# Cluster attention and two token mixers: idle matmuls among the first maxima, the second clusters' rows earlier, value products and row sums of group 0 regrouped

## The chip, the cores and the metric

The kernel runs on one NeuronCore of a Trainium2 chip. Its engines are TensorE (PE; PEld is its weight load), VectorE (DVE), ScalarE (ACT), GpSimd (POOL) and SyncE (SP, which issues the DMAs here). The metric is the device time of one launch in microseconds; smaller is better.

## The reference, cut to what matters

```python
# q, k, v: (2, 8, 768, 64); centroids: (8, 16, 64)
q_assign = argmax(q_n . c_n);  k_assign = argmax(k_n . c_n)       # cluster of each row
mask = q_assign[:, :, :, None] == k_assign[:, :, None, :]
scores = where(mask, (q @ k^T) / 8, -1e9)
attn = exp(scores - max(scores)); attn /= (sum(attn) + 1e-9)
x = (attn @ v), heads side by side                                # (2, 768, 512)
theta = x @ w_theta; y = w_tok_r @ (x cos theta) + w_tok_i @ (x sin theta)
u = x + y; x = u + relu(u @ w_ch)                                 # first mixer
u = x + (x^T U V)^T; out = u + relu(u @ w_ch1) @ w_ch2            # second mixer
```

## The kernel before, in words

The sixteen (batch, head) pairs are worked in eight groups of two heads. For a group g the inputs are loaded (`load_raw`), split into a high and a low part (`split_hi` L188 on ScalarE, `split_lo` L193 on GpSimd) and packed by sixteen DMAs (`pack`, L213) into the operands `qp` and `kp`. `assign_items` finds the clusters: similarities on TensorE (`sims` L121), then a transpose, a maximum (`amax` L128), four small operations and a transpose back on VectorE. The resulting one-hot rows become extra rows of `qp` and `kp`, by DMA (`mask_rows`, L161) or, for groups 0 and 1, directly through TensorE (`mask_direct`: products `oht` L174, copies on ScalarE L177, L179 and VectorE L181).

Row maxima come first: `max_pair(g, h, a)` multiplies two query tiles of head h with all keys, in three parts of one PSUM bank each (`smax` L251), and VectorE reduces each part (L255). `max_join` and `max_rows` put the maxima as rows into the second operand `qp[s, h, 1]`: a small product `mrow` (L281) and two ScalarE copies (L284). Only then can `scores_pair(g, h, a)` be finished: every part is a sum of two products, the second of them with `qp[s, h, 1]` (L303), and ScalarE takes its exponential (L308). `pv` multiplies with the values (L316) and `sum_keys(g, a)` gives half of the row sums (L335, then a transpose on VectorE, L338).

`prologue` does group 0's clusters, all its maxima and the scores of its head 0, and starts groups 1 and 2. Its function `heat(n)` issues n matmuls of 512 columns on a tile of zeros into a bank that nobody reads (L935). `attention` runs for each group six slots p = 0 to 5. In a slot stand the scores of group g, the maxima of group g + 1, and background work: `fill(t)` adds t to a debt `owed` and takes items from the queue `bg` (input split, pack, clusters of group g + 2; each with a cost), then weight conversion steps (`conv_step`; `magnitude` L385 on ScalarE waits for a weight block from HBM), until the debt is paid. t is 4.8 in the slots `BURST` = (2, 5) and 0.3 in the others. Value products and row sums stand in slots 2 and 5. `max_rows(g, 1)` stands in slot 2 of group g, behind the background work.

Each engine works its instructions in the order in which the code issues them. PSUM banks go round: `bank()` takes the one that was taken longest ago, and `give` returns those that were kept.

Of the kernel before, what the change touches and what calls it, by code (L numbers as in the profile page):

```python
# [41 lines left out]
def tile_cluster_block(ctx: ExitStack, tc: tile.TileContext, qk, v, cent, wth, wr, wi, wch,  # L42
                       u_in, v_in, w1, w2, cst, out):
    nc = tc.nc
# [194 lines left out]
    mx_t = {}  # L239
    THIRDS = [[(0, 0, 512)], [(0, 512, 256), (1, 0, 256)], [(1, 256, 512)]]  # L240

    def max_pair(g, h, a):

        s = g % SETS
        if a == 0:
            mx_t[g, h] = small.tile([P, 2 * NT], F32, tag="mx12", name="mx12")
        o = 2 * a
        for part in THIRDS:
            ps, c = bank("smax"), 0
            for j, k0, w in part:  # L250
                nc.tensor.matmul(out=ps[:, c:c + w], lhsT=qp[s, h, 0][:, (a + j) * P:(a + j + 1) * P],  # L251
                                 rhs=kp[s, h, 0][:, k0:k0 + w], start=True, stop=True)
                c += w
            n = len(part)
            nc.vector.tensor_reduce(mx_t[g, h][:, o:o + n], ps.rearrange("p (n w) -> p n w", n=n), axis=AX.X, op=ALU.max)  # L255
            o += n

    def max_join(g, h, act=False):
        mx = small.tile([P, NT], F32, tag="mx", name="mx")
# [68 lines left out]
    def sum_keys(g, a):  # L328

        ps = bank("l")  # L330
        for kt in range(3 * a, 3 * a + 3):
            for h in range(2):
                for hf in range(2):
                    o = 32 * (2 * h + hf)
                    nc.tensor.matmul(out=ps[o:o + 32, :HALF], lhsT=ones, rhs=pt[g, h, kt][:, cols(hf)],  # L335
                                     start=(kt == 3 * a), stop=(kt == 3 * a + 2))
        lt = slot("lt")[:, :HALF]
        nc.vector.transpose(lt, ps[:, :HALF])  # L338
        lsum[g, a] = lt
# [472 lines left out]
    assign = {}  # L812
# [21 lines left out]
    def attention():  # L834
# [1 line left out]

        ORDER = [(0, 0), (0, 2), (0, 4), (1, 0), (1, 2), (1, 4)]
        BURST = (2, 5)
        pvq = deque()
        held[0] = True  # L840

        def next_pv():
# [5 lines left out]
        for g in range(NG):  # L848
# [20 lines left out]
            if not nxt:  # L869
                for t in range(NP):  # L870
                    bg.append((1., lambda t=t: split_x(0, t, nc.gpsimd)))
            order = [(1, 0), None, (1, 2), None, (1, 4), None] if g == 0 else ORDER
            for p in range(NT):
                ready = len(pvq)
                if order[p]:
                    h, a = order[p]
                    scores_pair(g, h, a)
                    if h:
                        pvq.extend((g, kt, hf) for kt in (a, a + 1) for hf in range(2))
                if g == 0 and p < 2:  # L880
                    mask_direct(1, p, nc.scalar if p else nc.vector)
                if nxt:
                    max_pair(g + 1, p // 3, 2 * p % 6)
                    if p % 3 == 2:
                        max_join(g + 1, p // 3)

                while conv_after:
                    conv_after.popleft()()
                if p == 3 and g + 2 < NG:
                    mask_rows(g + 2)  # L890
                if g > 0 and p == 5:
                    bg.appendleft((.95, lambda: norm_x(g - 1)))
                    bg.appendleft((.97, lambda: spread(g - 1)))
                fill(2. if not nxt else 4.8 if p in BURST else .3)
                if not nxt:
                    if p == 0:
                        sum_keys(g - 1, 1)
                    if p == 2:
                        max_rows(g, 1)
                    if p == 5:  # L900
                        sum_keys(g, 0)
                    for _ in range(min(ready, (2, 2, 2, 0, 4, 4)[p])):
                        next_pv()
                elif p in BURST:
                    if p == 2 and g > 0:
                        max_rows(g, 1)
                        sum_keys(g - 1, 1)
                    if p == 5:
                        max_rows(g + 1, 0)
                        sum_keys(g, 0)  # L910
                    for _ in range(min(ready, 6)):
                        next_pv()
                    if p == 5 and g + 3 < NG:
                        (_, sims), *assign[g + 3] = assign_items(g + 3)
                        sims()
                if g > 0 and p == 2:
                    row_sums(g - 1)
# [9 lines left out]
    def prologue():  # L927
# [43 lines left out]
            for it in items:  # L971
                it[1]()

        its, its1 = assign_items(0), assign_items(1)
        for i in range(2):
            split_hi(0, i)
        split_lo(0, 0, nc.gpsimd)
# [10 lines left out]
        run(its[1:])  # L988
        run(its1[:1])
        mask_direct(0, 0, nc.vector)  # L990
        mask_direct(0, 1, nc.scalar)
        split_lo(0, 1, nc.gpsimd)
        pack_low(0, (0, 1))
        for i in range(2):
# [2 lines left out]
        pack_direct(1, 0)  # L997
        pack(1, main=(1,))
        pack_low(1, (0,))
        for a in (0, 2, 4):  # L1000
            max_pair(0, 0, a)
        max_join(0, 0, act=True)
        max_pair(0, 1, 0)
        max_pair(0, 1, 2)
        max_rows(0, 0)
        init_packs(2, nc.gpsimd)
        scores_pair(0, 0, 0)
        max_pair(0, 1, 4)
        max_join(0, 1)
        run(its1[1:])  # L1010
        scores_pair(0, 0, 2)
        heat(2)
        scores_pair(0, 0, 4)
        heat(2)
        max_rows(0, 1)
        its2 = assign_items(2)
        run(its2[:4])
        assign[2] = its2[4:]
        give("hot")

    def mixer():
# [171 lines left out]
```

## Time and profile before

| | us |
|---|---|
| median of 3 runs (684.31, 685.65, 945.77) | 685.65 |
| profiled execution, device time | 684.24 |
| its span in the trace | 682.4 |
| TensorE busy | 669.9 |
| VectorE busy | 464.7 |
| ScalarE busy | 348.6 |
| GpSimd busy | 272.0 |

The span is shorter than the device time by 1.84 us, which lies around it. The prologue ends at about 30 us, group 0 at 52.5, group 1 at 76.5; from there on TensorE has next to no idle time, so what an earlier stage loses or gains shows in full at the end.

### The profile page before, as it was taken

Reading aid. Unit: us, or ns where it says so; the run is one execution under the profiler, and the core shown is the slowest. Engines: PE = TensorE matmul, PEld = TensorE weight load, DVE = VectorE, ACT = ScalarE, POOL = GpSimd, SP = SyncE. Lnnn points to the kernel's source line nnn. Section 1 sums busy time; section 2 is a strip of 40 time slices with the busy share of each in tenths; the row PEclk is TensorE's granted clock in tenths of the full one; section 3 lists DMA queues with packets and bytes.
Section 4 is the critical chain, followed back from the end, with each engine's and each line's share of the span. In section 5 each row is a group of like instructions: output and inputs, shape, how many; then the busy total and the mean of one; then the engine's idle time right before and its main releaser. Section 6 shows DMA issues by size and latency. Waiting matters only on the chain.

```text
span 682.4 us, 11870 instructions
## 1 busy us (share of the span) xinstructions
PE 669.9 (98%) x4563; PEld 573.7 (84%) x4564; DVE 464.7 (68%) x832; ACT 348.6 (51%) x713; POOL 272.0 (40%) x277
## 2 busy tenths in 40 slices
PE   8899999999999999999999999999999999999997
PEld 3567766755765599999999999798899999999997
DVE  6888887897876366547374766777387765776554
ACT  8647656665776554455464442334354534543221
POOL 9423323223236333114234102348555765656321
PEclk9799999999999999999999999999999999999999
DMA  6769788476522102003120220112222211210013
GB/s 206 206 148 273 194 192 245 152 186 168 169 94 93 47 1 78 2 1 109 47 78 12 70 71 1 46 32 78 78 77 63 79 53 71 62 32 1 0 48 139
DMA packets 21833, 63.15 MB, mean 93 GB/s; under 512 B 4272, under 2 KB 7216, under 8 KB 21776
## 3 DMA queue, kind: packets, MB, share of 16 engines
q1 hardware_dynamic: 21776, 62.39, 31.3%
q8 instruction: 36, 0.59, 0.3%
q14 instruction: 21, 0.17, 0.1%
HBM read 40.94 MB, written 3.15 MB: 65 GB/s over the span
## 4 chain that ended last, share of the span: by engine, by line
PE 90%; ACT 5%; DVE 4%; DMA 1%; issue 1%; SPq 0%; ACTq 0%
PE y L562 15%; PE acc L801 15%; PE q L749 13%; PE pv L316 9%; PE st L303 8%; PE h L580 5%; PE l L335 5%; PE th L520 5%; PE acc L722 5%; PE g L703 4%; PE smax L251 3%; DVE mx L255 2%; ACT p L308 2%; PE h L631 2%; ACT hi L188 1%; PE th L524 1%
## 5 line engine op out<-in xcount | busy, mean ns | idle before, releaser
L401 POOL TENSOR_TENSOR wl<-cv,wh 128x768 fp32r<-128x768 f32 (+1 forms) x33 | 57.3, 1736 | 129.8 <-ACT wh L397 108.4
L255 DVE TENSOR_REDUCE mx<-smax 128x1 f32<-128x512 f32 x144 | 89.5, 680 | 21.9 <-PE smax L251 21.9
L308 ACT ACTIVATE p<-st 128x512 f32<-128x512 f32 x192 | 79.1, 513 | 44.5 <-PE st L303 43.7
L801 PE MATMUL acc<-g,wh 128*128 128x384 f32 x384 | 97.5, 334 | 0.0
L562 PE MATMUL y<-wh,z 128*128 128x384 f32 x384 | 87.6, 340 | 0.3 <-ACT z L540 0.3
L763 POOL TENSOR_TENSOR g<-sum,g 128x384 fp32r<-128x384 f32 x48 | 53.0, 1103 | 82.1 <-ACT g L762 76.2
L757 DVE TENSOR_TENSOR xT<-acc,xT 128x384 f32<-128x384 f32 x96 | 53.0, 555 | 42.0 <-PE acc L801 41.7
L303 PE MATMUL st<-qp,kp 128*128 128x256 f32 (+1 forms) x384 | 79.8, 350 | 0.4 <-ACT qp L284 0.2
L303 PEld LDWEIGHTS st<-qp,kp 128*128 128x128 f32 x384 | 58.6, 193 | 19.0 <-issue 8.5
L801 PEld LDWEIGHTS acc<-g,wh 128*128 128x128 f32 x384 | 69.4, 188 | 0.0
L562 PEld LDWEIGHTS y<-wh,z 128*128 128x128 f32 x384 | 66.9, 188 | 0.5 <-ACT z L540 0.5
L316 PE MATMUL pv<-p,v 128*32 128x384 f32 x768 | 66.2, 486 | 0.0
L761 ACT ACTIVATE sum<-sum 128x384 f32<-128x384 f32 x48 | 25.2, 524 | 78.5 <-DVE sum L757 78.5
L757 DVE TENSOR_TENSOR sum<-q,sum 128x384 f32<-128x384 f32 x84 | 45.5, 553 | 28.0 <-PE q L749 22.0
L801 PE MATMUL acc<-g,wl 128*128 128x384 f32 x192 | 64.1, 334 | 0.0
L316 PEld LDWEIGHTS pv<-p,v 128*32 128x32 f32 x768 | 31.5, 110 | 29.5 <-issue 20.9
L546 POOL TENSOR_TENSOR z<-tht,z 128x256 fp32r<-128x256 f32 x24 | 19.3, 803 | 86.2 <-ACT z L540 86.1
L392 DVE SCALAR_TENSOR_TENSOR cv<-cv,st 128x768 int32<-128x768 int32 (+2 forms) x47 | 50.4, 1072 | 3.0 <-ACT cv L385 2.6
L562 PE MATMUL y<-wl,z 128*128 128x384 f32 x192 | 48.8, 335 | 0.0
L251 PE MATMUL smax<-kp,qp 128*128 128x512 f32 x192 | 43.9, 347 | 3.0 <-ACT qp L177 1.9
L251 PEld LDWEIGHTS smax<-kp,qp 128*128 128x128 f32 x192 | 32.9, 191 | 12.9 <-issue 4.3
L385 ACT ACTIVATE cv<-st 128x768 f32<-128x768 f32 (+2 forms) x47 | 38.9, 827 | 5.3 <-POOL wl L475 3.6
(170 smaller groups left out, 1461.4 us busy)
## 6 DMA issues: line engine op xcount, KB each, us to landing
st<-in_w_dram SPq DMA_DIRECT2D x17, 512.0 KB, 3.4
st<-in_w_dram SPq DMA_DIRECT2D x10, 768.0 KB, 4.0
raw<-in_qk_dram SPq DMA_DIRECT2D x16, 384.0 KB, 4.8
qp<-hi SPq DMA_DIRECT2D x26, 192.0 KB, 2.9
st<-in_wr_dram SPq DMA_DIRECT2D x6, 768.0 KB, 4.5
st<-in_wi_dram SPq DMA_DIRECT2D x6, 768.0 KB, 4.2
kp<-hi SPq DMA_DIRECT2D x32, 96.0 KB, 3.1
qp<-lo SPq DMA_DIRECT2D x32, 96.0 KB, 2.8
```

The lines of the kernel that those rows point to most:

```text
L251: nc.tensor.matmul(out=ps[:, c:c + w], lhsT=qp[s, h, 0][:, (a + j) * P:(a + j + 1) * P], rhs=kp[s, h, 0][:, k0:k0 + w], start=True, stop=True)
L255: nc.vector.tensor_reduce(mx_t[g, h][:, o:o + n], ps.rearrange("p (n w) -> p n w", n=n), axis=AX.X, op=ALU.max)
L303: nc.tensor.matmul(out=ps[:, c:c + n], lhsT=kp[s, h, w][:, (a + j) * P:(a + j + 1) * P], rhs=qp[s, h, w][:, q0:q0 + n], start=(w == 0), st ...
L308: nc.scalar.activation(out=pt[g, h, a + j][:, q0:q0 + n], in_=ps[:, c:c + n], func=AF.Exp, scale=float(D) ** -0.5)
L316: nc.tensor.matmul(out=pvt[g][hf][r:r + 32, :HALF], lhsT=v_t[g][:, kt, r:r + 32], rhs=pt[g, r // 64, kt][:, cols(hf)], start=(kt == 0), st ...
L392: nc.vector.scalar_tensor_tensor(t, t, 3, self.lw, op0=ALU.logical_shift_left, op1=ALU.bitwise_or)
L401: nc.gpsimd.tensor_tensor(t[:, :c.w], c.t, f32(c.hi[:, :c.w]), op=ALU.subtract)
L562: nc.tensor.matmul(out=yps[u, j][hf][:, :HALF], lhsT=lhs, rhs=w[st][e][:, hf * HALF:(hf + 1) * HALF], start=(st == 0 and n == 0), stop=(st ...
L749: nc.tensor.matmul(out=ps[:, :HALF], lhsT=w[a][:, j * P:(j + 1) * P], rhs=u_block(self.b, y, e, j), start=(n == 0), stop=(n == 5))
L757: nc.vector.tensor_tensor(out, ps[:, :HALF], x, op=ALU.add)
L763: nc.gpsimd.tensor_tensor(t[:, 1], r, f32(t[:, 0]), op=ALU.subtract)
L801: nc.tensor.matmul(out=ps[:, :HALF], lhsT=wv[a], rhs=self.g[i, hf][:, x], start=(m == 0), stop=(m == 5))
```

## The change

In the prologue, four idle matmuls are put ahead of the first maxima and one behind each of twelve parts of the maxima of group 0; four idle matmuls between later scores go. The maximum of group 1's similarities is taken ahead of the first maxima, group 2's similarities ahead of `max_rows(0, 1)`. The scores (0, 1, 0) and the direct mask rows of group 1 move from group 0's first slots into the prologue. In group 0 the other scores stand in slots 1 and 3, four value products each in slots 1, 3 and 5, and both halves of the row sums in slots 3 and 5; group 1's slot 2 loses its row sums and value products.

```diff
--- before.py
+++ after.py
@@ -239,7 +239,7 @@
     mx_t = {}
     THIRDS = [[(0, 0, 512)], [(0, 512, 256), (1, 0, 256)], [(1, 256, 512)]]
 
-    def max_pair(g, h, a):
+    def max_pair(g, h, a, warmer=None):
 
         s = g % SETS
         if a == 0:
@@ -254,6 +254,8 @@
             n = len(part)
             nc.vector.tensor_reduce(mx_t[g, h][:, o:o + n], ps.rearrange("p (n w) -> p n w", n=n), axis=AX.X, op=ALU.max)
             o += n
+            if warmer:
+                warmer(1)
 
     def max_join(g, h, act=False):
         mx = small.tile([P, NT], F32, tag="mx", name="mx")
@@ -836,7 +838,7 @@
 
         ORDER = [(0, 0), (0, 2), (0, 4), (1, 0), (1, 2), (1, 4)]
         BURST = (2, 5)
-        pvq = deque()
+        pvq = deque((0, kt, hf) for kt in (0, 1) for hf in range(2))
         held[0] = True
 
         def next_pv():
@@ -869,7 +871,7 @@
             if not nxt:
                 for t in range(NP):
                     bg.append((1., lambda t=t: split_x(0, t, nc.gpsimd)))
-            order = [(1, 0), None, (1, 2), None, (1, 4), None] if g == 0 else ORDER
+            order = [None, (1, 2), None, (1, 4), None, None] if g == 0 else ORDER
             for p in range(NT):
                 ready = len(pvq)
                 if order[p]:
@@ -877,8 +879,6 @@
                     scores_pair(g, h, a)
                     if h:
                         pvq.extend((g, kt, hf) for kt in (a, a + 1) for hf in range(2))
-                if g == 0 and p < 2:
-                    mask_direct(1, p, nc.scalar if p else nc.vector)
                 if nxt:
                     max_pair(g + 1, p // 3, 2 * p % 6)
                     if p % 3 == 2:
@@ -901,14 +901,16 @@
                         sum_keys(g, 0)
                     for _ in range(min(ready, (2, 2, 2, 0, 4, 4)[p])):
                         next_pv()
-                elif p in BURST:
-                    if p == 2 and g > 0:
+                elif p in (BURST if g else (1, 3, 5)):
+                    if p == 2:
                         max_rows(g, 1)
-                        sum_keys(g - 1, 1)
+                        if g > 1:
+                            sum_keys(g - 1, 1)
                     if p == 5:
                         max_rows(g + 1, 0)
-                        sum_keys(g, 0)
-                    for _ in range(min(ready, 6)):
+                    if p == 5 or p == 3:
+                        sum_keys(g, int(g == 0 and p == 5))
+                    for _ in range(min(ready, 6 if g else 4)):
                         next_pv()
                     if p == 5 and g + 3 < NG:
                         (_, sims), *assign[g + 3] = assign_items(g + 3)
@@ -971,7 +973,7 @@
             for it in items:
                 it[1]()
 
-        its, its1 = assign_items(0), assign_items(1)
+        its, its1, its2 = assign_items(0), assign_items(1), assign_items(2)
         for i in range(2):
             split_hi(0, i)
         split_lo(0, 0, nc.gpsimd)
@@ -988,7 +990,9 @@
         run(its[1:])
         run(its1[:1])
         mask_direct(0, 0, nc.vector)
+        run(its1[1:2])
         mask_direct(0, 1, nc.scalar)
+        heat(4)
         split_lo(0, 1, nc.gpsimd)
         pack_low(0, (0, 1))
         for i in range(2):
@@ -997,25 +1001,26 @@
         pack_direct(1, 0)
         pack(1, main=(1,))
         pack_low(1, (0,))
-        for a in (0, 2, 4):
-            max_pair(0, 0, a)
+        max_pair(0, 0, 0)
+        max_pair(0, 0, 2, heat)
+        max_pair(0, 0, 4, heat)
         max_join(0, 0, act=True)
-        max_pair(0, 1, 0)
-        max_pair(0, 1, 2)
+        max_pair(0, 1, 0, heat)
+        max_pair(0, 1, 2, heat)
         max_rows(0, 0)
         init_packs(2, nc.gpsimd)
         scores_pair(0, 0, 0)
         max_pair(0, 1, 4)
         max_join(0, 1)
-        run(its1[1:])
+        run(its1[2:])
         scores_pair(0, 0, 2)
-        heat(2)
         scores_pair(0, 0, 4)
-        heat(2)
+        run(its2[:2])
         max_rows(0, 1)
-        its2 = assign_items(2)
-        run(its2[:4])
-        assign[2] = its2[4:]
+        scores_pair(0, 1, 0)
+        mask_direct(1, 0, nc.vector)
+        mask_direct(1, 1, nc.scalar)
+        assign[2] = its2[3:]
         give("hot")
 
     def mixer():
```

The first place is TensorE's order in the prologue behind the direct mask rows of group 0. Before:

```order
L174 LDWEIGHTS identb
L174 MATMUL oht<-eqw,identb 16x384
L251 MATMUL smax<-kp_87,qp_85 128x512
L251 MATMUL smax<-kp_87,qp_85 128x256 x2
L251 MATMUL smax<-kp_87,qp_85 128x512 x2
L251 MATMUL smax<-kp_87,qp_85 128x256 x2
L251 MATMUL smax<-kp_87,qp_85 128x512 x2
L251 MATMUL smax<-kp_87,qp_85 128x256 x2
L251 MATMUL smax<-kp_87,qp_85 128x512
L251 MATMUL smax<-kp_91,qp_89 128x512
```

Now (`hot` is the tile of zeros):

```order
L937 LDWEIGHTS hot
L937 MATMUL hot<-hot 128x512
L251 MATMUL smax<-kp_87,qp_85 128x512
L251 MATMUL smax<-kp_87,qp_85 128x256 x2
L251 MATMUL smax<-kp_87,qp_85 128x512 x2
L937 LDWEIGHTS hot
L937 MATMUL hot<-hot 128x512
L251 MATMUL smax<-kp_87,qp_85 128x256 x2
L937 LDWEIGHTS hot
L937 MATMUL hot<-hot 128x512
```

What moved: idle matmuls stand ahead of the first part and, from the second pair on, behind each part.

The second place is ScalarE's order in group 1, from slot 2's last exponential to slot 3's first (`hi` is the input split, `cv` a converted weight block, `mrow` the maxima rows, `xT` the copy of the value products). Before:

```order
L308 ACTIVATE p_820<-st 128x512
L385 ACTIVATE cv<-st 128x768
L284 ACTIVATE qp_98<-mrow 2x384 x2
L323 ACTIVATE xT_893<-pv 128x384 x2
L308 ACTIVATE p_908<-st 128x512
```

Now:

```order
L310 ACTIVATE p_832<-st 128x512
L188 ACTIVATE hi_0_863<-raw_0_514 128x768
L188 ACTIVATE hi_1_865<-raw_1_516 128x768
L387 ACTIVATE cv<-st 128x768
L286 ACTIVATE qp_98<-mrow 2x384 x2
L310 ACTIVATE p_919<-st 128x512
```

What moved: the two splits stood behind slot 0's exponentials; now they stand in slot 2, ahead of the copies of the maxima rows. The value products' copy is gone from here.

The third place is TensorE's order at the same point of group 1 (`l` are the row sums). Before:

```order
L281 MATMUL mrow<-identb,m_668 2x128
L335 MATMUL l<-p_404,ones 32x384 x2
L335 MATMUL l<-p_557,ones 32x384 x2
L335 MATMUL l<-p_422,ones 32x384 x2
L335 MATMUL l<-p_629,ones 32x384 x2
L335 MATMUL l<-p_423,ones 32x384 x2
L335 MATMUL l<-p_630,ones 32x384 x2
L316 MATMUL pv<-p_423,v_192 32x384 x2
L316 MATMUL pv<-p_630,v_192 32x384 x2
L316 MATMUL pv<-p_423,v_192 32x384 x2
L316 MATMUL pv<-p_630,v_192 32x384 x2
L303 MATMUL st<-qp_97,kp_99 128x512
```

Now:

```order
L283 LDWEIGHTS m_711
L283 MATMUL mrow<-identb,m_711 2x128
L305 MATMUL st<-qp_97,kp_99 128x512
L305 MATMUL st<-qp_98,kp_100 128x512
L305 MATMUL st<-qp_97,kp_99 128x256
L305 MATMUL st<-qp_98,kp_100 128x256
```

What moved: the row sums and value products between the maxima rows and the next scores are gone; they stand in group 0.

## Rows read from the trace of the kernel before

**Rows 1.** The page: span; busy time, share and count of each engine.
```profile
span 682.4 us, 11870 instructions
...
PE 669.9 (98%) x4563; PEld 573.7 (84%) x4564; DVE 464.7 (68%) x832; ACT 348.6 (51%) x713; POOL 272.0 (40%) x277
```

**Rows 2.** Stretches: start:end, length, busy per engine, granted clock, DMA share, GB/s.
```profile
13.30:19.50 6.20, 5.30 (x20) 3.17 (x20) 5.64 (x10) 4.87 (x9) 6.14 (x6) 1.00 0.90 292
19.60:26.30 6.70, 6.07 (x22) 4.60 (x23) 5.57 (x10) 3.02 (x8) 5.37 (x8) 0.50 0.95 207
...
33.10:34.30 1.20, 0.02 (x1) 0.05 (x1) 0.97 (x2) 1.18 (x3) 0.00 (x0) 1.00 0.00 0
```

**Rows 3.** Timeline, VectorE, maxima: start, length, operation, count, [idle before, releaser].
```profile
13.77 5.47 DVE L255 TENSOR_REDUCE mx<-smax 128x1 f32<-128x512 f32 x9 [0.72 <-PE smax L251]
...
24.48 1.89 DVE L255 TENSOR_REDUCE mx<-smax 128x1 f32<-128x512 f32 x3 [1.01 <-PE smax L251]
...
26.81 0.17 DVE L271 TENSOR_TENSOR m<-mx,m 128x6 bf16<-128x6 f32 x1
...
65.39 3.70 DVE L255 TENSOR_REDUCE mx<-smax 128x1 f32<-128x512 f32 x6
```

**Rows 4.** Timeline, TensorE: the prologue and group 0, same columns.
```profile
7.12 3.19 PE L935 MATMUL hot<-hot 128*128 128x512 bf16 x14
...
13.26 5.94 PE L251 MATMUL smax<-kp,qp 128*128 128x512 f32 x20 [0.71 <-ACT qp L177]
...
21.51 2.50 PE L303 MATMUL st<-qp,kp 128*128 128x512 f32 x7 [0.18 <-ACT qp L284]
...
30.36 1.97 PE L303 MATMUL st<-qp,kp 128*128 128x512 f32 x8
...
34.28 0.94 PE L251 MATMUL smax<-kp,qp 128*128 128x512 f32 x4 [1.20 <-ACT qp L177]
...
39.01 2.79 PE L316 MATMUL pv<-p,v 128*32 128x384 f32 x32
```

**Rows 5.** Chain of waits, end of group 0 and group 1: start, length, what.
```profile
51.82 0.65 PE sims L121 x8
...
54.75 1.40 PE st L303 x8
...
58.63 0.69 PE smax L251 x4
...
59.59 1.94 PE l L335 x22
61.53 1.29 PE pv L316 x16
62.82 1.15 PE st L303 x6
...
71.94 3.87 PE pv L316 x48
```

**Rows 6.** Timeline, ScalarE, group 1: exponentials, input split, weight block, maxima rows.
```profile
53.23 1.64 ACT L308 ACTIVATE p<-st 128x512 f32<-128x512 f32 x4 [6.18 <-PE st L303]
54.73 1.60 ACT L188 ACTIVATE hi<-raw 128x768 fp32r<-128x768 f32 x2
...
60.68 0.95 ACT L385 ACTIVATE cv<-st 128x768 f32<-128x768 f32 x1 [1.30 <-DMA st<-in_wth_dram]
61.53 0.96 ACT L284 ACTIVATE qp<-mrow 2x384 fp32r<-2x384 f32 x2
```

**Rows 7.** Timeline, SyncE's queue in group 1: packs and one-hot rows of group 3.
```profile
55.62 0.50 SPq L213 DMA_DIRECT2D qp<-hi  x1
...
68.99 0.60 SPq L213 DMA_DIRECT2D kp<-lo  x1
...
74.20 0.54 SPq L213 DMA_DIRECT2D kp<-oh  x1
```

**Rows 8.** DMA issues, 50 to 130 us: count, KB each, median us to landing.
```profile
kp<-oh SPq DMA_DIRECT2D x14, 24.0 KB, 1.9
```

## The prediction

> **What bounds the kernel now.** I read the page first: TensorE is busy 669.9 of 682.4 us [rows 1], so a gain must be TensorE time that is idle or slow now, or work that leaves it. The change only touches the prologue and groups 0 and 1, so I looked there, by stretches, and then engine by engine.
>
> Stretches [rows 2]: from 13.3 to 19.5 us the granted clock is 1.00, from 19.6 to 26.3 it is 0.50 (1.2 instead of 2.4 GHz), and from 33.1 to 34.3 TensorE is idle at 1.00. The timelines say why. In the first stretch VectorE sets the pace: nine reductions in 5.47 us, 0.608 each [rows 3], while a part costs TensorE far less; at the end of this loosely filled stretch the clock falls. In the second VectorE waits 1.01 us for TensorE ahead of the last three reductions [rows 3], and seven of the eight matmuls of a scores pair take 2.50 us [rows 4], against 1.40 for a whole pair at full clock [rows 5]; there the slow clock bounds. The third is 1.20 us in which the first maxima of group 1 wait for the copies of `mask_direct` [rows 4]. From 34.3 us on TensorE is full.
>
> **The change, part by part.**
>
> 1. *Idle matmuls.* Sixteen come, four go. Fourteen took 3.19 us at full clock [rows 4], 0.228 each. Behind a part they make 0.46 us of TensorE work where VectorE needs 0.608, so the twelve are hidden. If the clock fell all the same, part and idle matmul would take twice 0.46, 0.92, and the twelve could cost 12 x 0.31 = 3.7 us; that is the other end. The four ahead of the first part take 0.91 us where TensorE waits 0.71 now [rows 4]: +0.2.
>
> 2. *The clock in the prologue.* If it stays, VectorE's 1.01 us of waiting goes. The maxima of head 1, ready at 26.98 now [rows 3], are ready at 26.98 - 1.01 + 0.2 = 26.2. TensorE gets the last free bank at 24.48 - 1.01 + 0.2 = 23.7, finishes the last part at 23.9, then two pairs of scores at 1.40 and the similarities at 0.65 [rows 5]: 27.35. The maxima rows take some 0.2 and their ScalarE copies 0.96 [rows 6], to 28.6; nothing of TensorE covers this, since the similarities now stand ahead. Scores (0, 1, 0) need 1.2 more: 29.8, where they end at 30.36 + 1.97 = 32.33 now [rows 4]. Gain 2.5.
>
> 3. *Direct mask rows of group 1.* Four products take 34.28 - 1.20 - 32.33 = 0.75 us. Head 0's end at 30.55, and its copies let the maxima start 1.20 later, as now: 31.75. Head 1's four products fill 0.75 of this and no longer stand between the maxima. Up to the end of the first four value products there follow two pairs of maxima at 0.69, one of scores, the value products at 2.79 and the third pair of maxima: 31.8 + 6.26 = 38.05 instead of 41.80 [rows 4, 5]. Gain so far 3.75.
>
> 4. *The rest of group 0.* One pair of scores 1.40, three of maxima 2.07, maxima rows 0.2, row sums twice 1.94, eight value products 5.58, similarities 0.65: 13.8 us, to 51.85 instead of 52.47 [rows 5]. That is 0.6 earlier, with 1.94 + 1.29 us of work taken over from group 1.
>
> 5. *Group 1, slot 2.* The work that left it stood between the maxima rows and scores (1, 1, 0), whose second product needs these rows through ScalarE. `fill` now owes 0.56 less when group 1 begins, so the two input splits move from slot 0 into slot 2, ahead of these copies. ScalarE, worked out: scores of slot 2 end at 51.85 + 3 x 1.40 + 2 x 0.69 = 57.4; the last exponential ends 0.8 later [rows 5, 6], 58.25; splits 1.60, to 59.85; the weight block's copy, 0.95, can start at 60.68 at the latest, when the block is there now, and at 59.85 at best; the maxima rows' copies take 0.96 [rows 6]. So the rows are there between 61.75 and 62.55; I take 62.2. TensorE is done with the product for them at 58.3, adds one first product, and then stands for 3.7 us. This new wait swallows the moved work.
>
> 6. *To the end of group 1.* From the second product on there remain 1.2 + 0.69 + 1.40 + 0.69 + 1.40 + 0.69 of scores and maxima, 0.2, row sums 1.94, six value products 3.87 and similarities 0.65: 12.7 us, to 74.95. Now group 1 ends at 71.94 + 3.87 + 0.65 = 76.46 [rows 5]. VectorE starts slot 3's reductions at 65.39 now [rows 3]; without one row-sum transpose and the weight shift ahead of them at about 64.6, just in time for the banks. **Gain 1.5.** Later groups have the same work for TensorE, and there row sums and six value products cover the copies.
>
> Whether the clock outlives the wait of step 5 is open. The nearest row on idleness is the 1.20 us at 33.1, with the clock at 1.00 during it and full work behind [rows 2]; the nearest on the clock is the fall after a stretch with 5.30 of 6.20 us busy. Going by the idle row, the sum stands. The Trainium skill, "TensorE: Matmul & The Clock Gate", Part 1, says that "the default state is throttled, and activity releases the throttle"; by that rule a stretch without matmuls speaks against this change, and the time would be that of rival A. No row here shows an idle stretch of 3.7 us.
>
> **The sum.** The profiled execution took 684.24 us, 1.84 of it outside the span. 684.24 - 1.5 = 682.7. The two close runs lie 0.07 and 1.41 above the profiled one; I add 0.6 for where a median falls: **683.3**. Its own range, from the ends of step 5 and this spread: 682.0 to 684.6.
>
> **Rivals.** Their times stand against the profiled execution's 684.24, as the 682.7 does; for a median the same 0.6 comes on top.
>
> A. *The new wait costs the clock.* TensorE stands 3.7 us in slot 2 of group 1 and goes on at half speed. Such a stretch lasted 6.7 us here [rows 2]; half of it is lost, 3.4, if all of it falls on work, and about 1.7 if half falls on the wait. 684.4 to 686.1, **slower than before** by up to 1.9. For it: the clock fell here even while work went on. Against: it outlived 1.20 us. It decides if a granted clock of 0.50 follows the wait. Chance 0.33.
>
> B. *No such wait*: the copies come earlier than I think. Then VectorE is next: slot 4's third part waits for a bank until 65.2, and 9.0 us remain, to 74.2: 682.0. Without either wait group 1 would end 58.3 + 12.9 = 71.2, 5.3 early: 679.0. Against: the order on ScalarE. Chance 0.12.
>
> C. *The idle matmuls don't hold the clock* in the prologue, so the change misses its first aim. Then step 2's 2.5 is lost, of which the weight block's arrival gives back about 0.5: 684.7; with the idle matmuls at half speed up to 3 more, 687.7. For it: around 20 us TensorE still waits for the maxima rows, as now. Against: the stretch ahead is filled twice as densely. Chance 0.12.
>
> D. *Late packs.* The splits start at 58.25 instead of 54.73, 3.5 later, with POOL's low parts and sixteen DMAs on SP behind them. Head 0's last one-hot row for group 2's first maxima is issued at 74.20 now [rows 7], with the maxima due at 76.46 + 1.40 = 77.9. Shifted in full it is issued at 77.7; with 1.9 us to land [rows 8] and its own 0.5 that is 80.1, against 74.95 + 1.40 = 76.35: a wait of up to 3.8, up to 686.5. Against: fourteen issues from 55.62 to 68.99 took 13.4 us at some 0.6 each, so some 5 us of it were waits, and a later start finds earlier transfers landed. Chance 0.06.
>
> **How the numbers follow.** The forecast has 0.37. Cases above and below 684.2 are about even. With the 0.6, A ends at 686.7; the range 681.0 to 686.8 takes in the forecast, A, the lower parts of C and D and the upper half of B. A measurement of this kernel tells about 2 per cent, 13.7 us, from no change; all cases lie within it. I leave 0.01 for faster by more, 0.02 for slower by more, 0.97 for within.
>
> **What would show it.** Right: granted clock 1.00 from 19.6 to 26.3; no wait of VectorE near 24; group 0's end near 51.9; a wait of TensorE of 3 to 4 us for `mrow` copies (L286) in group 1, with ScalarE busy on splits and a weight block; its end near 75. Wrong: a clock of 0.50 behind that wait (A) or near 20 us (C); maxima of group 2 waiting for one-hot rows (D); group 1 ending near 72 to 74 (B).

## The result, and the profile after

The changed kernel takes 688.13 us (median of 6 runs, 687.24 to 689.2), the kernel before 684.76 in the same session (median of 6 too, one of them 945.77). The ratio is 1.0055, 95% interval 1.0041 to 1.0069: half a per cent slower, and above the top of the predicted range, 686.8. The profiled execution took 689.09 us. Its page (span, then busy time of each engine; answers to [rows 1]):

```profile
span 687.3 us, 11903 instructions
...
PE 673.1 (98%) x4575; PEld 580.3 (84%) x4576; DVE 470.9 (69%) x832; ACT 349.5 (51%) x713; POOL 271.1 (39%) x277
```

Shares of busy time say nothing here: TensorE reads 98% in both. What helps is to cut the trace at matmuls that both kernels have, and to compare stretch by stretch. Times are starts in the two traces: of the first `smax`, of group 1's first `smax`, of the `sims` that close group 0, group 1 and group 4, and of the first matmul of `theta`.

| stretch, us | before | after | difference |
|---|---|---|---|
| start to first maxima | 13.26 | 14.93 | +1.67 |
| to group 1's first maxima | 21.02 | 19.00 | -2.02 |
| to the end of group 0 | 17.29 | 19.91 | +2.62 |
| group 1 | 23.94 | 24.89 | +0.95 |
| groups 2 to 4 | 79.83 | 79.49 | -0.34 |
| groups 5 to 7, up to theta | 80.41 | 82.27 | +1.86 |
| sum | 235.75 | 240.49 | +4.74 |

The first line is a late start. Of the fourteen idle matmuls ahead of everything the first seven start about 0.43 us apart in this execution and the rest 0.22; together they take 4.66 us instead of 3.2 [rows 4]. (The profile's granted clock reads 1.00 over both, so it doesn't settle why.) Four of the eleven experiments start late too. Among the nine kernels with the changed prologue five start late and four early (first maxima at 13.15 to 13.41); the other four kernels traced are all early, so the traces can't rule out that the prologue makes a late start more likely. The four new idle matmuls ahead of the first maxima cost nothing that can be seen: the early kernels with them begin their maxima at 13.15 to 13.41, those without at 13.13 to 13.35. Medians mix early and late starts, stretches don't: so the stretches are what I compare.

The prologue does what it should. Stretches (start:end, length, busy time of PE, PEld, DVE, ACT, POOL, granted clock, DMA share, GB/s), two of them those of [rows 2]:

```profile
13.30:19.50 6.20, 6.09 (x33) 3.34 (x29) 6.01 (x11) 6.15 (x11) 5.11 (x5) 1.00 0.87 285
19.60:26.30 6.70, 5.83 (x32) 3.66 (x32) 6.38 (x14) 3.05 (x9) 6.42 (x9) 1.00 0.84 189
...
64.30:68.00 3.70, 3.67 (x13) 3.13 (x14) 3.49 (x6) 1.75 (x4) 1.30 (x1) 0.62 0.85 204
```

The clock holds at 1.00 (2.4 GHz) from 19.6 to 26.3, where it was 0.50. The third line is new: 0.62 behind a wait in group 1. TensorE's timeline (start, length, engine, line, operation, count, [idle before, releaser]; the first rows answer to [rows 4]):

```profile
7.55 4.66 PE L937 MATMUL hot<-hot 128*128 128x512 bf16 x14
...
14.93 1.17 PE L251 MATMUL smax<-kp,qp 128*128 128x512 f32 x5
...
23.03 1.43 PE L305 MATMUL st<-qp,kp 128*128 128x512 f32 x7 [0.32 <-ACT qp L286]
...
30.57 1.42 PE L305 MATMUL st<-qp,kp 128*128 128x512 f32 x7 [0.70 <-issue]
...
33.93 0.94 PE L251 MATMUL smax<-kp,qp 128*128 128x512 f32 x4 [0.33 <-ACT qp L177]
...
61.36 0.50 PE L305 MATMUL st<-qp,kp 128*128 128x512 f32 x1
64.33 1.82 PE L305 MATMUL st<-qp,kp 128*128 128x512 f32 x7 [2.47 <-ACT qp L286]
65.95 1.48 PE L251 MATMUL smax<-kp,qp 128*128 128x512 f32 x4
67.23 2.18 PE L305 MATMUL st<-qp,kp 128*128 128x512 f32 x8
```

Seven score matmuls take 1.43 us at 23.03 instead of 2.50. At 64.33 stands the forecast wait for the copies of the maxima rows. It came about in the predicted way, on ScalarE behind the splits and a weight block (answers to [rows 6]):

```profile
61.06 1.60 ACT L188 ACTIVATE hi<-raw 128x768 fp32r<-128x768 f32 x2
62.53 0.91 ACT L387 ACTIVATE cv<-st 128x768 f32<-128x768 f32 x1
63.32 0.96 ACT L286 ACTIVATE qp<-mrow 2x384 fp32r<-2x384 f32 x2
```

But the chain of waits of group 1 (start, length, what) does not run through it:

```profile
60.73 1.90 DVE mx L255 x3
...
62.85 1.01 DVE m L272
...
63.88 1.75 DVE m L273
...
69.26 1.15 DVE mx L255 x2
...
70.46 1.80 PE st L305 x8
```

It goes through VectorE, and through two instructions on 128x6 elements that took 0.18 and 0.17 us elsewhere. VectorE's timeline, then GpSimd's:

```profile
62.65 0.17 DVE L262 TENSOR_REDUCE mx<-mx 128x6 f32<-128x12 f32 x1
62.85 1.00 DVE L272 CAST m<-mx 128x6 bf16<-128x6 f32 x1
63.88 1.75 DVE L273 TENSOR_TENSOR m<-mx,m 128x6 bf16<-128x6 f32 x1
...
69.18 3.61 DVE L255 TENSOR_REDUCE mx<-smax 128x1 f32<-128x512 f32 x6
```

```profile
62.01 3.59 POOL L193 TENSOR_TENSOR lo<-raw,hi 128x768 fp32r<-128x768 f32 x2 [21.74 <-ACT hi L188]
```

GpSimd's two low parts run from 62.01 to 65.60, some 1.8 us each. The cast ends at 63.85, about where the first ends, and the subtraction at 65.63, where the second does: VectorE waits for GpSimd, 0.82 + 1.58 = 2.4 us. The Trainium skill, "SBUF — State Buffer", section "Who interferes with whom", says that VectorE and GpSimd share a pair of ports, that a VectorE instruction with two SBUF inputs contends with a GpSimd instruction that reads SBUF, and that casts can contend too, while reductions don't. The rows agree. The second head's reductions begin at 69.18 instead of 65.39 [rows 3]: 3.8 later, of which 2.4 are this wait; group 0 had ended 2.3 later, late start included.

### The profile page after: what moved, and what is told of

It is laid out like the page before. It is cut to its first block, busy times and chain, and to the rows that moved or that the text cites. A ratio compares the mean times of both kernels' runs of the same rounds, so it can differ in the third digit from the quotient of the medians.

```text
span 687.3 us, 11903 instructions
## 1 busy us (share of the span) xinstructions
PE 673.1 (98%) x4575; PEld 580.3 (84%) x4576; DVE 470.9 (69%) x832; ACT 349.5 (51%) x713; POOL 271.1 (39%) x277
## 4 chain that ended last, share of the span: by engine, by line
PE 89%; DVE 5%; ACT 3%; issue 1%; POOL 1%; DMA 1%; SPq 0%; ACTq 0%; POOLq 0%; DVEq 0%
PE y L564 15%; PE acc L803 15%; PE q L751 13%; PE pv L318 8%; PE st L305 8%; PE h L582 5%; PE th L522 5%; PE acc L724 5%; PE l L337 4%; PE g L705 4%; PE smax L251 3%; DVE mx L255 2%; PE h L633 2%; ACT p L310 1%; PE sims L121 1%
## 5 line engine op out<-in xcount | busy, mean ns | idle before, releaser
L318 PEld LDWEIGHTS pv<-p,v 128*32 128x32 f32 x768 | 37.0, 110 | 24.1 <-issue 10.0
L394 DVE SCALAR_TENSOR_TENSOR cv<-cv,st 128x768 int32<-128x768 int32 (+2 forms) x47 | 48.9, 1041 | 2.0 <-ACT cv L387 1.3
L251 PE MATMUL smax<-kp,qp 128*128 128x512 f32 x192 | 45.9, 358 | 1.7 <-DVE lt L340 0.6
L193 POOL TENSOR_TENSOR lo<-raw,hi 128x768 fp32r<-128x768 f32 x16 | 29.3, 1851 | 38.3 <-ACT hi L188 28.1
```

The costliest lines, as they stand in the source:

```text
L318: nc.tensor.matmul(out=pvt[g][hf][r:r + 32, :HALF], lhsT=v_t[g][:, kt, r:r + 32], rhs=pt[g, r // 64, kt][:, cols(hf)], start=(kt == 0), st ...
L394: nc.vector.scalar_tensor_tensor(t, t, 3, self.lw, op0=ALU.logical_shift_left, op1=ALU.bitwise_or)
```

## The experiments

Each is the changed kernel with an edit, unless it says otherwise. "The account" is `owed`, the background work that `fill` still has to give out (us). The change leaves 0.56 more work to group 0's budget, so from there on all background work stands later in the program. The cut of every trace, in the stretches of the table above (one trace of each kernel):

| kernel | median us | first maxima | to gr. 1's maxima | gr. 0 | gr. 1 | gr. 2-4 | gr. 5-7 |
|---|---|---|---|---|---|---|---|
| before | 684.1 to 684.8 | 13.26 | 21.02 | 17.29 | 23.94 | 79.83 | 80.41 |
| after | 688.13 | 14.93 | 19.00 | 19.91 | 24.89 | 79.49 | 82.27 |
| e1_debt | 685.12 | 13.21 | 19.12 | 22.00 | 22.27 | 79.78 | 80.39 |
| e2_before_debt | 690.0 | 13.33 | 20.73 | 18.92 | 26.16 | 79.47 | 82.20 |
| e3_rows_first | 690.78 | 14.77 | 18.99 | 19.90 | 26.69 | 79.50 | 82.22 |
| e5_no_idle | 689.26 | 13.35 | 20.06 | 19.91 | 24.88 | 79.53 | 82.26 |
| e6_debt_g1 | 684.7 | 13.15 | 19.02 | 19.91 | 23.99 | 79.81 | 80.39 |
| e7_zero_low | 687.91 | 14.94 | 18.97 | 19.90 | 24.12 | 79.53 | 82.25 |
| e8_before_idle | 682.52 | 13.13 | 19.22 | 17.29 | 23.94 | 79.83 | 80.41 |
| e9_debt_g2 | 686.18 | 13.41 | 19.05 | 19.89 | 25.36 | 79.87 | 80.41 |
| e10_g1_rows_first | 683.59 | 13.18 | 19.01 | 19.89 | 22.30 | 79.81 | 80.41 |
| e12_both_gone | 685.91 | 15.10 | 19.00 | 19.90 | 22.50 | 79.75 | 82.28 |
| e13_no_regroup | 683.66 | 14.89 | 18.98 | 19.49 | 22.91 | 79.81 | 80.41 |

**e1_debt**: the account put right from the start.

```diff
-    owed = [0.]
+    owed = [.56]
```

> The changed kernel with the background debt starting at 0.56 instead of 0, so that from group 1 on the input splits stand in slot 0 again, as before the change; nothing else differs. Theory (the loss is the moved splits: ScalarE's copies of the maxima rows wait behind them and VectorE's small bfloat16 operations wait for GpSimd's low parts): the 2.5 us wait for the maxima rows in group 1 shrinks below 1, no VectorE cast of 6 columns takes over 0.3 us in slot 2 of group 1, groups 5 to 7 lose nothing more; 3 to 5 us faster than the changed kernel, 0 to 2 faster than the kernel before. Rival (taking row sums and value products out of group 1's slot 2 is what costs): the wait stays near 2.5 us, within 1 us of the changed kernel. Second rival (idle matmuls or the prologue cost): no change against the changed kernel either.

685.12 us, ratio to before 1.0006 (0.9994 to 1.0018). TensorE's row, VectorE's and GpSimd's:

```profile
63.56 1.44 PE L305 MATMUL st<-qp,kp 128*128 128x512 f32 x7 [1.23 <-ACT qp L286]
```

```profile
34.63 2.19 DVE L132 TENSOR_TENSOR eqw<-s_t,mxc 128x384 bf16<-128x384 f32 x1
36.86 1.87 DVE L138 TENSOR_TENSOR eqw<-eqw,cvals 128x384 bf16<-128x384 bf16 x1
...
59.28 3.81 DVE L255 TENSOR_REDUCE mx<-smax 128x1 f32<-128x512 f32 x6
...
63.53 0.17 DVE L273 TENSOR_TENSOR m<-mx,m 128x6 bf16<-128x6 f32 x1
```

```profile
34.57 3.94 POOL L193 TENSOR_TENSOR lo<-raw,hi 128x768 fp32r<-128x768 f32 x2 [9.55 <-issue]
58.30 3.65 POOL L193 TENSOR_TENSOR lo<-raw,hi 128x768 fp32r<-128x768 f32 x2 [19.79 <-ACT hi L188]
```

Group 1 is 2.6 us shorter and groups 5 to 7 are as before. TensorE's wait is 1.23, not below 1 as expected, and against the kernel before nothing is gained. In group 1 the low parts now stand beside reductions, which are not held up: six take 3.81 us beside them, 0.63 each, as without. In exchange group 0 is 2.1 longer: there the low parts now stand beside two cluster steps, 2.19 and 1.87 us instead of 0.55 and 0.36. The account decides which VectorE instructions meet GpSimd.

**e2_before_debt**: the kernel before with the change's shift of the account alone.

```diff
-    owed = [0.]
+    owed = [-.56]
```

> The kernel before with the debt starting at -0.56, so that the splits move into slot 2 there too, with row sums and value products still behind the maxima rows. Theory: the shift alone costs about 1 to 3 us, by VectorE waiting for GpSimd in slot 2 of group 1 and by the conversion steps of the last groups standing elsewhere. Rival (only the missing cover costs): within 0.7 us of the kernel before.

690.0 us, ratio 1.0084 (1.0066 to 1.0102). Nothing is moved out of group 1 here, its row sums and value products cover the copies but for 0.76 us, and yet it grows from 23.94 to 26.16, with the same two instructions held up:

```profile
62.06 1.02 DVE L270 CAST m<-mx 128x6 bf16<-128x6 f32 x1
63.11 1.74 DVE L271 TENSOR_TENSOR m<-mx,m 128x6 bf16<-128x6 f32 x1
```

TensorE then waits 1.71 us for VectorE (at 68.66). The granted clock is 1.00 throughout group 1, so the clock has no part in this. The shift alone costs at least as much as the whole change, and more than the 1 to 3 us expected; 1.6 of it lie in group 0.

**e3_rows_first**: in slot 2 of group 1, the maxima rows ahead of the background work.

```diff
+                early = g == 1 and p == 2
+                if early:
+                    max_rows(g, 1)
                 fill(2. if not nxt else 4.8 if p in BURST else .3)
...
-                        max_rows(g, 1)
+                        if not early:
+                            max_rows(g, 1)
```

> The changed kernel with max_rows(1, 1) issued ahead of the background work in slot 2 of group 1 alone, so that ScalarE's copies of the maxima rows pass the splits; the splits and GpSimd's low parts stay in slot 2. If ScalarE's order is the whole cost of group 1: 2 to 2.5 us faster than the changed kernel. If VectorE's wait for GpSimd bounds behind it: TensorE's wait for the rows goes, but the wait for a free bank of the next maxima takes its place, and under 1 us is gained.

690.78 us, ratio 1.009 (1.0072 to 1.0108): slower still, which neither reading expected. TensorE's wait for the copies shrinks to 0.65, but GpSimd's low parts, now from 63.08 to 67.04, catch the next two-input instructions (VectorE, then TensorE):

```profile
63.60 1.74 DVE L132 TENSOR_TENSOR eqw<-s_t,mxc 128x384 bf16<-128x384 f32 x1
65.38 1.87 DVE L138 TENSOR_TENSOR eqw<-eqw,cvals 128x384 bf16<-128x384 bf16 x1
```

```profile
69.97 0.49 PE L251 MATMUL smax<-kp,qp 128*128 128x512 f32 x1 [3.22 <-DVE mx L255]
70.56 2.56 PE L305 MATMUL st<-qp,kp 128*128 128x512 f32 x8
```

TensorE waits 3.22 us for VectorE instead, and the slow clock follows (eight score matmuls in 2.56 us).

**e5_no_idle**: without the sixteen idle matmuls.

```diff
-        heat(4)
...
-        max_pair(0, 0, 2, heat)
+        max_pair(0, 0, 2)
...
```

> The changed kernel without its sixteen idle matmuls in the prologue (neither the four ahead nor the twelve among the first maxima). Theory: the clock falls near 20 us and VectorE waits about 1 us there for TensorE, so 1.5 to 3 us slower than the changed kernel. Rival (the idle matmuls only cost): 0 to 1 us faster.

689.26 us, ratio 1.0076 (1.0056 to 1.0096). The stretch up to group 1's maxima is 1.06 longer, TensorE again at half clock:

```profile
21.45 2.50 PE L305 MATMUL st<-qp,kp 128*128 128x512 f32 x7 [0.32 <-ACT qp L286]
```

The idle matmuls are worth about 1.1 us in the changed prologue by the traces, less than the 1.5 to 3 expected.

The run shows one thing more. In group 1 stands the same wait for the copies, but the clock stays up behind it:

```profile
63.81 1.44 PE L305 MATMUL st<-qp,kp 128*128 128x512 f32 x7 [2.47 <-ACT qp L286]
...
69.34 0.49 PE L251 MATMUL smax<-kp,qp 128*128 128x512 f32 x1 [1.53 <-DVE mx L255]
```

The granted clock is 1.00 from 63.8 to 67.5, against 0.62 in the changed kernel. Yet group 1 takes 24.88 us, against 24.89: the cast and the subtraction take 1.00 and 1.75 us here too, and what TensorE gains by the clock it spends waiting for VectorE, 1.53 us. So in the changed kernel the slow clock lengthens group 1 by nothing that can be seen; VectorE's chain, with its wait for GpSimd, is enough to keep it there.

**e6_debt_g1**: the account put right when group 1 begins, so that group 0 keeps its places.

```diff
             if g == 1:
+                owed[0] += .56
```

> The changed kernel, with the 0.56 us of owed background work given back at the start of group 1 (group 0 keeps the changed kernel's places). Theory 1 (VectorE waiting for GpSimd sets the end of group 1, because the account puts GpSimd's low parts beside VectorE's small instructions): group 0 as in the changed kernel (first maxima to its last signature scores 19.9 us, against 22.0 where the debt was given back from the start), group 1 as where the debt was given back from the start (22.3 us between the two groups' signature scores, casts of the maxima 0.17 us), nothing lost in groups 5 to 7: 1 to 2 us less than that kernel's 685.1, so 683 to 684, at or below the kernel before. Theory 2 (the regrouping of value products and row sums itself costs it, whatever the account): about 685, as with the debt from the start, or more.

684.7 us, ratio 1.0003 (0.999 to 1.0017). Theory 1 was half right. Group 0 stays at 19.91, nothing is held up on VectorE, groups 5 to 7 are as before. But group 1 takes 23.99, not 22.3. ScalarE's row of the weight block, then TensorE's:

```profile
60.59 0.89 ACT L387 ACTIVATE cv<-st 128x768 f32<-128x768 f32 x1 [0.84 <-DMA st<-in_wth_dram]
61.39 0.96 ACT L286 ACTIVATE qp<-mrow 2x384 fp32r<-2x384 f32 x2
```

```profile
62.40 1.44 PE L305 MATMUL st<-qp,kp 128*128 128x512 f32 x7 [2.32 <-ACT qp L286]
...
64.84 2.65 PE L305 MATMUL st<-qp,kp 128*128 128x512 f32 x8
```

Group 1 begins 2.25 us earlier than in e1_debt. So the weight block's transfer now ends after ScalarE is ready for it, the rows' copies queue behind, TensorE waits 2.32 instead of 1.23, and the clock falls: eight score matmuls in 2.65 us. The clock does not fall in every execution of this kernel: over a whole run it reads 1.000 in five of the twelve (683.07 to 684.93 us) and 0.996 to 0.998 in seven (684.45 to 686.69), the traced one among them.

**e7_zero_low**: GpSimd writes zeros in place of group 3's low parts, so it does not read there.

```diff
-        eng.tensor_tensor(t, raw[g, i], f32(hl[g, i, 0]), op=ALU.subtract)
+        if g == 3:
+            eng.memset(f32(t), 0.0)
+        else:
+            eng.tensor_tensor(t, raw[g, i], f32(hl[g, i, 0]), op=ALU.subtract)
```

> The changed kernel, but GpSimd writes zeros in place of group 3's two low parts (the subtraction is left out, so GpSimd reads nothing there); all else, the account too, stands as in the changed kernel. Theory 1 (VectorE waits for GpSimd while that reads): the cast and the subtraction of the maxima at about 62.9 take 0.17 us each instead of 1.00 and 1.75, the reductions of the second head's maxima start near 66.8 instead of 69.2, group 1 is 2.0 to 2.4 us shorter, time 685.7 to 686.2 against the changed kernel's 688.1. Theory 2 (TensorE's wait for ScalarE's copies of the maxima rows, 2.47 us, and the clock that falls behind it set the end): ScalarE's order is the same, group 1 as long as before, 687.8 to 688.5.

687.91 us, ratio 1.0047 (1.0032 to 1.0062). The zeros wait for nothing and are written at 40.2, so GpSimd is idle beside the casts. VectorE and TensorE:

```profile
62.81 0.18 DVE L275 CAST m<-mx 128x6 bf16<-128x6 f32 x1
63.02 0.17 DVE L276 TENSOR_TENSOR m<-mx,m 128x6 bf16<-128x6 f32 x1
...
67.06 1.89 DVE L258 TENSOR_REDUCE mx<-smax 128x1 f32<-128x512 f32 x3 [0.25 <-PE smax L254]
```

```profile
64.27 2.33 PE L308 MATMUL st<-qp,kp 128*128 128x512 f32 x7 [2.45 <-ACT qp L289]
```

VectorE's 2.4 us are gone, as theory 1 expected; group 1 gets only 0.77 shorter, as theory 2 would have it. Now TensorE's wait of 2.45 and the clock behind it (seven score matmuls in 2.33) set the pace; e12_both_gone takes this wait away as well. Neither theory alone was right.

**e12_both_gone**: e3_rows_first and e7_zero_low together.

```diff
+        if g == 3:
+            eng.memset(f32(t), 0.0)
...
+                if early:
+                    max_rows(g, 1)
...
```

> The changed kernel with both edits: the maxima rows are turned and copied ahead of the background work in slot 2 of group 1, and GpSimd writes zeros in place of group 3's low parts (the subtraction is left out). Each edit alone left group 1 at 24.1 us (zeros; TensorE's 2.45 us wait and the half clock behind it stay) and 26.7 us (rows first; VectorE's 1.2 and 1.5 us behind GpSimd stay), against 24.9 in the changed kernel. If the two waits stand side by side and each alone is enough to set the end: with both gone group 1 takes 22.0 to 22.6 us (VectorE's own work is then the bound, as in the kernel with the debt given back from the start, 22.3), time 685.3 to 686.2. If a third thing sets it (transfers of the packs or the conversions): 23.9 or more, 687 or more.

685.91 us, ratio 1.0021 (1.0011 to 1.0032). This closes a square. Group 1, in us:

| | low parts subtracted | zeros instead |
|---|---|---|
| rows behind the background work | 24.89 | 24.12 |
| rows first | 26.69 | 22.50 |

One edit alone gains 0.77 or loses 1.8; both gain 2.4. The two waits stand side by side, and either is enough to keep group 1 near 24 or above. The cell of 26.69 is not quite the changed kernel less one wait: with the rows first, GpSimd meets other, longer instructions of VectorE (e3_rows_first).

**e9_debt_g2**: the account put right only when group 2 begins.

```diff
             if g == 2:
+                owed[0] += .56
```

> The changed kernel, with the 0.56 us of owed background work given back only at the start of group 2. Group 1 as in the changed kernel (VectorE's casts 1.00 and 1.75 us, group 1 3.2 us later than before). If the waits of TensorE in groups 5 to 7 (0.7 twice, 0.35, 0.47) come from conversion steps that the account has moved there: they go, 686.3 to 686.8. If they follow from group 1's lateness: 688.1 as the changed kernel.

686.18 us, ratio 1.0028 (1.0018 to 1.0038). Group 1 keeps its trouble (25.36), groups 5 to 7 are back at 80.41: the 1.86 us lost there came from the account too. In the changed kernel these waits of TensorE stood there, and are absent here:

```profile
164.23 1.76 PE L305 MATMUL st<-qp,kp 128*128 128x512 f32 x8 [0.66 <-ACT p L310]
...
191.85 1.70 PE L251 MATMUL smax<-kp,qp 128*128 128x512 f32 x4 [0.35 <-DVE mx L255]
224.21 2.85 PE L305 MATMUL st<-qp,kp 128*128 128x512 f32 x15 [0.47 <-ACT qp L286]
```

The middle one stands behind such an instruction of VectorE again, though no run takes this one apart: a weight step took 2.20 us instead of 0.96, beside a low part of the weights on GpSimd from 188.54 to 190.38. VectorE's row of the changed kernel:

```profile
189.00 2.20 DVE L394 SCALAR_TENSOR_TENSOR cv<-cv,st 128x768 int32<-128x768 int32 x1
```

Such a step is not new with the change: one of 2.21 us stands at 198.10 in the kernel before and at 200.34 here, with two waits of TensorE behind it, 0.28 and 0.26. What the account changes is its place. Against this run the changed kernel loses about 0.55 at the first place, 0.55 net at the second and 0.75 at the third.

**e8_before_idle**: the kernel before with idle matmuls behind its first maxima, nothing else.

```diff
...
-        for a in (0, 2, 4):
-            max_pair(0, 0, a)
+        max_pair(0, 0, 0)
+        max_pair(0, 0, 2, heat)
+        max_pair(0, 0, 4, heat)
...
-        max_pair(0, 1, 0)
-        max_pair(0, 1, 2)
+        max_pair(0, 1, 0, heat)
+        max_pair(0, 1, 2, heat)
```

> The kernel before with the change's sixteen idle matmuls among the first maxima and nothing else of the change. If the prologue's gain is the clock's and lasts: VectorE's wait of 1.01 us at 24.5 goes, the seven score matmuls take 1.4 instead of 2.5 us, group 0 ends 1.0 to 1.8 us sooner, 682.5 to 683.3. If something later swallows it (the account is the same as before, so nothing moves): 684.2, as the kernel before.

They are twelve: the expectation counts sixteen, but the four ahead of the first maxima are not in this kernel. 682.52 us, ratio 0.9978 (0.9967 to 0.999): faster than both kernels. VectorE's last nine reductions run through, where before it waited 1.01 us [rows 3]; TensorE's scores are at full clock:

```profile
19.67 5.46 DVE L255 TENSOR_REDUCE mx<-smax 128x1 f32<-128x512 f32 x9
```

```profile
21.23 1.44 PE L305 MATMUL st<-qp,kp 128*128 128x512 f32 x7 [0.33 <-ACT qp L286]
```

The 1.8 us of the prologue reach the end: every later stretch is as before, to 0.02.

**e10_g1_rows_first**: e6_debt_g1 with e3_rows_first's edit.

```diff
             if g == 1:
+                owed[0] += .56
...
+                if early:
+                    max_rows(g, 1)
...
```

> The changed kernel with the debt given back at the start of group 1 and, in slot 2 of group 1, the maxima rows turned and copied ahead of the background work, so that the copies no longer queue on ScalarE behind a conversion that waits for its transfer until 60.6. If that wait (2.32 us) and the clock behind it are what keeps group 1 at 24.0 us there: 22.0 to 22.5 us, time 682.7 to 683.3. If VectorE sets it in any case (in the kernel with the debt given back from the start it works without a gap from 57.0 to 72.5, and group 1 takes 22.3): the same 22.3. If neither: 24.0, 684.7.

683.59 us, ratio 0.9995 (0.9986 to 1.0003). Group 1 is down to 22.30, as both readings expected, so the run doesn't tell them apart; the time is 0.3 above the expected range. VectorE then works without a gap from 57.05 to 74.62, and TensorE waits 0.65 for the copies and once for VectorE:

```profile
65.52 0.49 PE L251 MATMUL smax<-kp,qp 128*128 128x512 f32 x1 [0.77 <-DVE mx L255]
```

**e13_no_regroup**: the changed prologue and the account put right in group 1, but value products and row sums in the slots where the kernel before has them. The scores of group 0 stay in slots 1 and 3, and since the queue of value products starts with four, group 0 works twelve of them (six and six), not ten.

```diff
             if g == 1:
+                owed[0] += .56
...
-                elif p in (BURST if g else (1, 3, 5)):
+                elif p in BURST:
...
-                        if g > 1:
+                        if g > 0:
                             sum_keys(g - 1, 1)
...
-                    if p == 5 or p == 3:
-                        sum_keys(g, int(g == 0 and p == 5))
+                    if p == 5:
+                        sum_keys(g, 0)
...
```

> The changed kernel without its regrouping: in group 0 value products in slots 2 and 5 and the first row sums in slot 5 as in the kernel before, its second row sums back in slot 2 of group 1; prologue as changed; the debt given back at the start of group 1. If the regrouping is what takes the prologue's gain away (group 1 without cover for its copies): groups 0 and 1 together about 41 to 42 us against 43.9 with the regrouping, 682.2 to 683.2, as the kernel before with the idle matmuls alone (682.5). If it is the reordered prologue or the account: 684 or more.

683.66 us, ratio 0.9994 (0.9985 to 1.0003). Group 0 and 1 together take 42.4 us: 1.5 less than e6_debt_g1, but 1.2 more than e8_before_idle. Above the expected range by half a microsecond, and the run does not decide between its readings. The trace shows where group 0 pays: its last three pairs of maxima stand with no scores or value products between them and take 3.52 us at VectorE's pace (nine reductions in 5.43), where a pair takes 0.69 elsewhere [rows 5], and the row sums wait 0.26 for VectorE. With the two value products more (1.29) and the mask rows moved out (0.75) that is the 2.2 us by which its group 0 exceeds the 17.29 of e8_before_idle.

## Why the prediction was wrong

The forecast would have theta begin at 235.75 - 1.5 = 234.25; it began at 240.49. Of the 6.2 us between them 1.7 are this execution's late start, 0.5 the prologue, 0.7 group 0, 1.8 group 1 and 1.5 the groups behind it. The steps, in order:

1. *Idle matmuls hidden*: right. The maxima with them run at VectorE's pace; the four ahead, put at 0.2, cost nothing that can be seen.
2. *The clock in the prologue*: right, and measured alone in e5_no_idle and e8_before_idle. Its end was 0.5 late: scores (0, 1, 0) end at 31.99, 30.3 without the late start, not at 29.8. The 0.70 us of idle TensorE ahead of them are the wait for the copies, which the sum had; it ended 0.3 late, and the seven matmuls behind it took 1.42 us, not 1.2.
3. and 4. *Group 0*: right within 0.7. The steps make it 1.9 longer (2.5 earlier at its first maxima, 0.6 at its end); it grew by 2.62, to 19.91 us. 17.29, with the 1.94 + 1.29 moved in and 0.75 of direct mask rows moved out, is 19.77. One cluster step was held up by GpSimd, 1.99 us instead of 0.36, without effect on TensorE.
5. *The new wait*: the mechanism was right (splits, weight block, then the rows' copies on ScalarE), the size 2.47 us instead of 3.7. **Rival A happened**: behind the wait the clock was 0.62 of full over 3.7 us. But it did not set the time: in e5_no_idle the clock stays at 1.00 behind the same wait, and group 1 is as long (24.88). In e7_zero_low, where VectorE is not held up, wait and clock leave group 1 at 24.12, against the forecast's 23.1. The rule cited there ("the default state is throttled, and activity releases the throttle") fits four of five traces: waits of 2.3 to 2.5 us were followed by the slow level in the changed kernel, e6_debt_g1, e7_zero_low and e9_debt_g2, but not in e5_no_idle; one of 1.23 in e1_debt was not either. What tells e5_no_idle from the others stays open.
6. *To the end of group 1*: **this step failed.** It has VectorE start slot 3's reductions "at about 64.6, just in time for the banks"; they started at 69.18, 4.6 later, of which 1.7 are the late start and 2.4 the wait for GpSimd. I had followed the splits onto ScalarE, and in rival D onto the DMA queue, but not asked what GpSimd's low parts, which move with them, would stand beside on VectorE. No rival held this. Before, they ran from 55.67 to 59.34, beside reductions alone.

The same step failed for the later groups as well. It says of them that "row sums and six value products cover the copies". Against the copies they do; but 0.56 us less owed also moves the weights' conversion steps, in every group up to the end, and that cost 1.86 us in groups 5 to 7 (e9_debt_g2). I treated the account as a matter of group 1 only.

Taken together: the prologue gains 2.0 us of the 2.5 forecast; the account takes 1.86 in groups 5 to 7 and, with what the regrouping uncovers, 4.2 in group 1 (24.89 instead of 23.94 less the 3.23 of work that left). With the account right and the rows first (e10_g1_rows_first) the change is level with the kernel before. There the 3.23 us that leave group 1 shorten it by only 1.64, since VectorE's work and two short waits remain, while group 0 grows by 2.6. Moving the work is no gain even without the accidents: e8_before_idle, which moves none of it, has the better ratio, 0.9978 against 0.9995.

## What to carry to other kernels

When an edit changes how much background work a planner still owes, list what moves on every engine to the end of the loop, GpSimd too, and look at what stands beside it. Two waits side by side hide each other: taking one away can show nothing or even a loss, and only the run with both gone prices them. Where one part of a change works in the profile (here the idle matmuls), run it alone on the old kernel.

## What the runs showed of the hardware

- A cast and a subtraction of 128x6 elements took 1.00 and 1.75 us instead of 0.18 and 0.17, a weight step 2.20 instead of 0.96, the first two ending where a GpSimd subtraction of some 1.8 us ends, the third 0.8 behind it. Reductions from PSUM beside the same GpSimd work kept 0.63 us.
- Behind waits of TensorE of 2.3 to 2.5 us the clock fell from 2.4 towards 1.2 GHz in four kernels (granted 0.62, 0.54 and 0.50 over the next 3.7 us in the changed kernel, e7_zero_low and e9_debt_g2; in e6_debt_g1 0.55 from 64.8 to 67.5). Behind 2.47 us in e5_no_idle, and 1.23 in e1_debt, it stayed at 1.00: the length of the wait alone does not decide it.
- The start of the program spreads between executions: with the same work up to there, the fourteen idle matmuls took 3.20 us (e6_debt_g1) or 4.66 (the changed kernel), and the first maxima began at 13.15 to 15.10.
